# Idle products, load order, first-state banks and the order of three phases in a chunked attention + GELU-MLP kernel

## The chip, the cores and the metric

The kernel runs on one core of a Trainium2 chip. The metric is the device time of one launch in microseconds (us), from the run's start to its end on that core. The median of three runs of the kernel before is 209.88 us (209.52 to 210.0). Times inside a run are counted in us from the start of the profiled span.

## The reference

Linear attention with a per-head decay `lam`, followed by a two-layer MLP with an exact GELU. The attention output, laid out as 3072 tokens by 512 features, is the MLP's input.

```python
# q, k, v: (4 batches, 8 heads, 768, 64);  block = 64
for b in range(nb):
    intra = einsum('bhic,bhjc->bhij', qb, kb) * Dmask        # lam**(i-j) for i >= j
    intra = einsum('bhij,bhjd->bhid', intra, vb)
    inter = einsum('bhid,bhde->bhie', qb * lam_pow, kv_state)
    out[:, :, sl] = intra + inter
    kv_state = lam_block * kv_state + einsum('bhsd,bhse->bhde', kb * rev_pow, vb)
x = out.transpose(0, 2, 1, 3).reshape(3072, 512)
return gelu_exact(x @ w_in) @ w_out                          # 512 -> 2048 -> 512
```

## The kernel before

**Tiling.** The kernel works on chunks of 128 positions, six groups g = 0 to 5, each with all 4 batches (512 tokens). For each group it computes scores, masked scores, attention outputs and the state for the next group, then the first MLP product with GELU (`mm1`, 16 feature tiles of 128) and the second one (`mm2`). Groups overlap: while the MLP of group g runs, the attention of group g+1 is made. From group 2 on, the MLP products are Strassen-like: seven products in place of eight, from sums of blocks of `x`, `w_in`, `gelu` and `w_out` that VectorE makes.

**What sets the order.** Nothing is reordered by a scheduler. The kernel is recorded in the order in which its Python runs, and each engine executes its own instructions in that order, with semaphores between the engines. The order comes from strings of letters that `script` (L676) walks, one action for each word:

- `LOADS1` (L673) is the order of the DMA loads of the opening, all issued by the POOL engine. Capital V, K, Q with 0 or 1 are the halves ("pairs" of batches) of group 0; small letters those of group 1; `i0` to `i7` are eight slices of `w_in` (256 features each, `load_w_in` L109), `w0` to `w7` eight slices of `w_out` (`load_w_out` L112). `s0` and `s1` are multiplications on POOL that scale the values of pair 0 and 1 (`scale_v` L194). The halves K0 and Q0 are loaded ahead of all (L119, L120). Each pair load is two DMAs.
- `HEAD` (L674) is the work of the opening: `.` is one idle product (`keep_warm` L687: a 128x128 by 256 matmul on zeros, whose result nobody reads); `K`, `Q` transpose a pair's keys or queries on TensorE into PSUM and copy them out (`p_transposes` L308); `S` makes half of a pair's scores and masks them on VectorE (`p_scores` L326, masks L353); `O` makes a pair's outputs and scales them into `x` (`p_outputs` L356, `p_x` L371 with the VectorE product L374); `m` and `n` are the mm1 blocks of pair 0 and of pair 1 (`mm1_part` L692: eight matmuls, then GELU on ACT), in the order of slices 0, 4, 1, 5, 2, 6, 3, 7; `z` makes the first state (`p_state_products` L379, matmuls L389, VectorE L396); `g` makes ACT load the GELU table.
- `PHASE1` (L758): sixteen mm2 blocks of group 0 (`p`, `mm2_plain` L497, four rounds over four PSUM banks), sums of `w_in` and `w_out` on VectorE (`i`, `w`, `t`), and the attention of group 1 (`k`, `q`, `s`, `o`; `h` scales values on ACT).
- `PHASE2` (L777): mm1 of group 1 (`m`, `n`), attention of group 2, the states (`z`, `Z`, decay `y`, `Y` on ACT), loads of group 3 (`K`, `V`, `Q`), and the sums of `x` (`x`).
- `L2S` (L776) has sixteen digits: how many mm1 blocks later each of the sixteen VectorE sums of GELU blocks in phase 2 is recorded (`later` L63, `tick` L67).

**PSUM.** The eight banks are named by tags: uY, uV, uZ (mm1 blocks in turn), mY, mR, a0, a1, a2. A bank is free again when its reader on VectorE or ACT is done; the next writer on TensorE waits for that. The state products `z` take two banks given by their tags.

Of the kernel before, what the change touches and what calls it, by code (L numbers as in the profile page):

```python
# [14 lines left out]
def kernel(  # L15
# [11 lines left out]
    B, H, S, D = q.shape  # L27
# [20 lines left out]
    V, A, P, G, SY = nc.vector, nc.scalar, nc.tensor, nc.gpsimd, nc.sync  # L48

    def bank(tag, shape, dtype=F32, name=None):  # L50
        return ps.tile(shape, dtype, tag=tag, name=name or "p_" + tag, bufs=1)
# [4 lines left out]
    def need(*keys):  # L56
        for key in keys:
            assert key in done, key
# [28 lines left out]
    def load(g, pair, name):  # L87
        if pair == 0:
            raw[g, name] = raw_pool.tile([128, B, H, D], BF16, tag="r" + name, name="raw_" + name, bufs=1 if name == "q" else 2)
        t = raw[g, name].rearrange("p (n a) h d -> p n (a h d)", n=2)[:, pair].rearrange("p (h t d) -> p h t d", h=H, t=2)  # L90
        for b in range(2):
            G.dma_start(t[b * 64:(b + 1) * 64].rearrange("p h t d -> p h (t d)"),
                        dram[name][2 * pair + b, :, g * C:(g + 1) * C, :].rearrange("h (p t) d -> p h (t d)", t=2))
        raw[g, pair, name] = t
# [57 lines left out]
    for hi in range(2):  # L152
        p = slice(hi * D, (hi + 1) * D)
# [32 lines left out]
    def new_x(g):  # L186
        xs[g] = x_pool.tile([128, HP, B, C], BF16, tag="x", name="x_t")
# [191 lines left out]
    def p_state_products(g, tags):  # L379
        if g > 0:  # L380
            need(*[("vs", g, h) for h in range(H)])
        done.add(("sp", g))
        kv = [bank(t, [128, 2, HP, D]) for t in tags]
        for pair in range(2):
            for hp in range(HP):
                for t in range(2):
                    for b, hi in ((0, 0), (1, 1), (1, 0), (0, 1)):
                            r = slice(b * 64, (b + 1) * 64)
                            P.matmul(kv[b][hi * D:(hi + 1) * D, pair, hp, :], raw[g, pair, "k"][r, 2 * hp + hi, t, :],  # L389
                                     vs[g, pair][r, 2 * hp + hi, t, :], start=(pair == 0 and hp == 0 and t == 0),  # L390
                                     stop=True, skip_group_check=True)
        states[g + 1] = work.tile([128, B, HP, D], BF16, tag="state", name="state")
        if g == 0:
            lam_c_b = lam_c[:, None, :, None].to_broadcast((128, 2, HP, D))
            for b in range(2):
                V.tensor_mul(states[1][:, b::2], kv[b], lam_c_b)  # L396
            done.add(("st", 1))
        else:
            raw["tmp", g] = work.tile([128, B, HP, D], F32, tag="tmp", name="tmp", bufs=1)
            for b in range(2):  # L400
                V.tensor_add(raw["tmp", g][:, b::2], kv[b], states[g][:, b::2])
# [5 lines left out]
    def new_g(g):  # L407
        gts[g] = g_pool.tile([128, NK2, T], BF16, tag="g", name="g_t")
# [261 lines left out]
        return slots  # L670


    LOADS1 = "V0 K1 i0 Q1 i4 i5 i1 i2 V1 s0 i6 i3 w4 q0 i7 s1 w2 w0 k0 w1 k1 v0 w5 q1 w7 w6 v1 w3"  # L673
    HEAD = "b . . . . . . . . . . . . . . . . . . . . . . . Q K . . S S g . . . . . . O Q K m S m S m m m O z n n m m n n n n n m n"  # L674

    def script(text, actions):  # L676
        for word in text.split():
            fn = actions[word]
            (fn.pop(0) if isinstance(fn, list) else fn)()
# [12 lines left out]
    def mm1_part(g, i, pair, lag=None):  # L692

        need(*[("x", g, 2 * pair + b) for b in range(2)])
        h = bank(tags[part_no[0] % 3], [128, 2, 256])
        part_no[0] += 1
        x = xs[g].rearrange("p k s c -> p k (s c)")
        w = slice(256 * pair, 256 * pair + 256)
        for j in range(2):
            kf = 2 * i + j  # L700
            for ki in range(NK1):
                P.matmul(h[:, j, :], w_in_t[:, ki, kf * 128:(kf + 1) * 128], x[:, ki, w],  # L702
                         start=(ki == 0 and j == 0), stop=True, skip_group_check=True)
        A.activation(gts[g][:, 2 * i:2 * i + 2, w], h, ACT.Gelu)
        done.add(("gp", g, i, pair))
        u = i % 4
        if lag and all(("gp", g, x, y) in done for x in (u, u + 4) for y in range(2)):
            done.update(("g", g, u, n) for n in "XYZW")
            for n, j in enumerate((1, 2, 4, 3)):
                later(int(lag[4 * u + n]), lambda j=j: sums_g(g, u, j))  # L710
        tick()

    new_x(0)
    new_g(0)
    for item in LOADS1.split():
        i = int(item[1:])
# [6 lines left out]
        else:  # L723
            load(int(item[0].islower()), i, item[0].lower())
    script(HEAD, {
        ".": keep_warm,
# [6 lines left out]
              lambda: (p_outputs(0, 1, 0, ("a2", "a0")), p_outputs(0, 1, 1, None), p_x(0, 1, 0), p_x(0, 1, 1))],  # L733
        "m": [lambda i=i: mm1_part(0, i, 0) for i in (0, 4, 1, 5, 2, 6, 3, 7)],
        "n": [lambda i=i: mm1_part(0, i, 1) for i in (0, 4, 1, 5, 2, 6, 3, 7)],
        "z": lambda: p_state_products(0, ("a1", "a2")),
    })


# [15 lines left out]
        "z": lambda: p_state_products(1, ("a0", "a1")),  # L755
        "y": lambda: decay(2, raw["tmp", 1]),
    }
    PHASE1 = "i i p w i k q p p p w i p s q k w t p p s p t p w s o p p p h h p s p p o p"  # L758
    script(PHASE1, attn_1)


# [11 lines left out]
    new_g(1)  # L773
    new_gs(1)
    new_x(2)
    L2S = "2242369401781123"  # L776
    PHASE2 = "q z m k y n s q m n k K s h n m s V o m Q n n s t t M h c m n o c c x c x m x x m Z n m n Y"  # L777

    def digits(text, i, n):
        return [int(c) for c in text[i * n:(i + 1) * n]]  # L780

    script(PHASE2, {
        "m": [lambda i=i: mm1_part(1, i, 0, L2S) for i in (0, 4, 1, 5, 2, 6, 3, 7)],
        "n": [lambda i=i: mm1_part(1, i, 1, L2S) for i in (0, 4, 1, 5, 2, 6, 3, 7)],
        "w": attn_1["w"],
# [27 lines left out]
    for g in range(2, NG):  # L813
# [17 lines left out]
        for c in seqs:  # L831
# [6 lines left out]
            elif c == "v":  # L838
                i = visits.pop(0)
# [5 lines left out]
            elif c == "c":  # L845
                x = cross.pop(0)
                if g + 2 < NG:
                    crossbar(g + 2, *x)
            elif c == "h":
                h = heads.pop(0)  # L850
                if att:
                    scale_v_group(g + 1, h)
            elif c == "x":
                i = sums.pop(0)
# [38 lines left out]
```

## Time and profile before

| | |
|---|---|
| median of 3 runs | 209.88 us (209.52 to 210.0) |
| the profiled execution's own time | 210.69 us |
| its span, first to last instruction | 208.9 us |
| mean granted TensorE clock | 0.975 |
| TensorE (PE) busy | 196.9 us, 94% |
| VectorE (DVE) busy | 143.2 us, 69% |
| ScalarE (ACT) busy | 120.4 us, 58% |
| GpSimd (POOL) busy | 57.9 us, 28% |

How to read it: PE is the matmul stream, PEld the weight loads that overlap with it, POOL also issues the loads, SP the stores. The page's second part cuts the span into 40 slices of 5.2 us and gives the busy share of each engine in tenths; PEclk is the clock that TensorE was granted, in tenths of full speed. The views by windows give busy us and instruction counts (x) for chosen stretches. The timeline gives start and duration of merged groups of instructions, with the idle time before them and what ended it in brackets. The chain of waits follows the work that ended last back to its start.

### The profile page before, as it was taken

The numbers are of one execution on the slowest core, as the hardware profiler recorded it, in microseconds if no ns is written. First come the engines' busy times: TensorE is split into PE (matmuls) and PEld (weight loads), VectorE is DVE, ScalarE is ACT, GpSimd is POOL, SyncE is SP. The second block draws the span as 40 slices with busy tenths as digits, with TensorE's granted clock in tenths as the row PEclk, the third lists the DMA queues.
The fourth block names the chain that finished last, engine by engine and source line by source line (L and its number), as shares of the span: only waits on it lengthen the run. The fifth ranks groups of instructions, "written<-read, shape, count | busy, mean of one in ns | idle before, by whom it ended". The sixth has DMA issues, their size and how long they took to land.

```text
span 208.9 us, 6157 instructions
## 1 busy us (share of the span) xinstructions
PE 196.9 (94%) x2639; PEld 158.8 (76%) x2639; DVE 143.2 (69%) x290; ACT 120.4 (58%) x245; POOL 57.9 (28%) x70
## 2 busy tenths in 40 slices
PE   7459899999999998999999999999999999999992
PEld 5337688554678887888888888888888888888881
DVE  1872495688567996798988498796699654665140
ACT  5524446355479858872589663788455556665201
POOL 7978886775071302700035000000000000000000
PEclk9785999999999999999999999999999999999999
DMA  5999999999789945999929996330002030022123
GB/s 56 139 177 191 195 195 190 192 179 164 151 143 155 136 82 99 99 157 120 211 77 149 155 132 126 103 100 3 0 27 80 2 100 3 0 72 81 51 83 117
DMA packets 81274, 23.46 MB, mean 112 GB/s; under 512 B 69472, under 2 KB 80736, under 8 KB 81248
## 3 DMA queue, kind: packets, MB, share of 16 engines
q0 software_dynamic: 62416, 13.64, 74.3%
q1 hardware_dynamic: 18832, 9.44, 20.6%
q8 instruction: 20, 0.33, 0.7%
q14 instruction: 6, 0.05, 0.1%
HBM read 27.27 MB, written 6.29 MB: 161 GB/s over the span
## 4 chain that ended last, share of the span: by engine, by line
PE 89%; ACT 3%; DVE 2%; DMA 2%; issue 1%; POOL 1%; DVEq 0%; ACTq 0%; POOLq 0%
PE p_mY L665 15%; PE p_uY L521 14%; PE p_mR L665 13%; PE p_uV L521 7%; PE p_uV L702 5%; PE p_uY L702 5%; PE p_uZ L702 4%; PE t_ps L314 4%; PE p_uZ L521 3%; DMA raw_q<-in_q_dram 2%; PE p_a L269 2%; PE p_a L241 2%; PE p_uY L501 2%; PE p_a L347 2%; PE p_uZ L501 2%; PE p_uV L501 2%
## 5 line engine op out<-in xcount | busy, mean ns | idle before, releaser
L665 PEld LDWEIGHTS <-g_t 128*128 128x128 bf16 x320 | 31.1, 98 | 4.2 <-issue 0.4
L521 PEld LDWEIGHTS <-s_in 128*128 128x128 bf16 x256 | 24.5, 97 | 5.5 <-issue 2.2
L702 PEld LDWEIGHTS <-w_in_t 128*128 128x128 bf16 x256 | 24.8, 101 | 4.3 <-issue 0.3
L665 PEld LDWEIGHTS <-gs 128*128 128x128 bf16 x240 | 23.3, 98 | 2.9
L665 PE MATMUL p_mY<-w_out_t,g_t 128*128 128x256 bf16 x160 | 20.8, 273 | 0.2 <-ACT o_q L648 0.2
L521 PEld LDWEIGHTS <-w_in_t 128*128 128x128 bf16 x192 | 18.5, 98 | 2.8
L521 PE MATMUL p_uY<-tx,s_in 128*128 128x256 bf16 x128 | 19.2, 272 | 1.0 <-ACT p_uV L543 1.0
L533 ACT ACTIVATE g_t<-p_uV 128x512 bf16<-128x512 f32 x16 | 9.5, 594 | 17.6 <-PE p_uV L521 17.4
L571 DVE TENSOR_TENSOR p_uZ<-p_uY,Vs 128x512 f32<-128x512 f32 x16 | 11.2, 699 | 10.6 <-PE p_uY L521 10.4
L353 DVE TENSOR_TENSOR sc_m<-p_a,m_p 128x512 bf16<-128x512 f32 x20 | 12.9, 686 | 6.3 <-PE p_a L347 6.2
L259 DVE TENSOR_TENSOR sc_m<-p_a,m_p 128x512 bf16<-128x512 f32 x24 | 15.6, 683 | 1.1 <-PE p_a L244 1.1
L533 ACT ACTIVATE g_t<-Vs 128x512 bf16<-128x512 f32 x16 | 10.0, 628 | 10.1 <-DVE Vs L580 10.1
L580 DVE TENSOR_TENSOR Vs<-p_uY,Vs 128x512 f32<-128x512 f32 x16 | 11.0, 691 | 6.9 <-PE p_uY L521 6.7
L98 POOL DMA_DIRECT2D raw_q<-in_q_dram x3 | 5.1, 1704 | 32.5 <-DMA qT<-raw_q 32.5
L471 DVE TENSOR_TENSOR gs<-g_t 128x512 bf16<-128x512 bf16 x20 | 8.4, 420 | 8.0 <-ACT g_t L533 7.9
L702 PE MATMUL p_uY<-x_t,w_in_t 128*128 128x256 bf16 x88 | 12.3, 286 | 0.0
L702 PE MATMUL p_uV<-x_t,w_in_t 128*128 128x256 bf16 x88 | 12.2, 285 | 0.0
L665 PE MATMUL p_mR<-t_out,gs 128*128 128x256 bf16 x80 | 11.4, 273 | 0.0
L665 PE MATMUL p_mR<-w_out_t,g_t 128*128 128x256 bf16 x80 | 11.2, 273 | 0.0
L543 ACT COPY p_uV<-p_uY 128x512 f32<-128x512 f32 x16 | 9.2, 572 | 3.3 <-PE p_uY L521 3.2
L665 PE MATMUL p_mR<-w_out_t,gs 128*128 128x256 bf16 x80 | 11.0, 273 | 0.0
L551 ACT COPY Vs<-p_uV 128x512 f32<-128x512 f32 x16 | 9.4, 588 | 2.5 <-PE p_uV L521 2.5
(125 smaller groups left out, 434.9 us busy)
## 6 DMA issues: line engine op xcount, KB each, us to landing
w_in_t<-in_moe_w_in_dram POOLq DMA_DIRECT2D x8, 256.0 KB, 7.6
w_out_t<-in_moe_w_out_dram POOLq DMA_DIRECT2D x8, 256.0 KB, 6.9
raw_k<-in_k_dram POOLq DMA_DIRECT2D x12, 128.0 KB, 6.2
raw_q<-in_q_dram POOLq DMA_DIRECT2D x12, 128.0 KB, 5.7
raw_v<-in_v_dram POOLq DMA_DIRECT2D x12, 128.0 KB, 6.3
raw_k<-in_k_dram POOLq DMA_DIRECT2D x3, 512.0 KB, 10.6
raw_v<-in_v_dram POOLq DMA_DIRECT2D x3, 512.0 KB, 12.0
raw_q<-in_q_dram POOLq DMA_DIRECT2D x3, 512.0 KB, 9.5
```

What stands on the lines that cost most here:

```text
L259: V.tensor_mul(sc_m[g, s_sc][:, :, r, :], sc[r], m_nh[:, r])
L353: V.tensor_mul(sc_m[g, pair][half][:, :, hi], sc[hi], m_ph[:, hi, 2 * half:2 * half + 2])
L471: eng.tensor_add(s1, gLH, gHH)
L501: P.matmul(mo[io], gts[g][:, kf, io * C:(io + 1) * C], w_out_t[:, kf, :], start=(part == 0 and j == 0), stop=(part == 3 and j == 3))
L521: P.matmul(dst[:, b, :], w(ko, f0 + b * 128), x_of(ko), start=(start and b == 0 and ko == 0), stop=True, skip_group_check=True)
L533: A.activation(dst, src, ACT.Gelu)
L543: A.copy(st["V"], st["Y"])
L551: A.copy(st["Vs"], st["V"])
L571: V.tensor_add(st["Z"], st["Y"], st["Vs"])
L580: V.tensor_add(st["Vs"], st["Y"], st["Vs"])
L665: P.matmul(st[dst][:, io, :], a(kf, io), b(kf), start=(new and u == 0 and io == 0 and kf == 0), stop=True, skip_group_check=True)
L702: P.matmul(h[:, j, :], w_in_t[:, ki, kf * 128:(kf + 1) * 128], x[:, ki, w], start=(ki == 0 and j == 0), stop=True, skip_group_check=True)
```

## The change

Five edits in the opening and the two phases behind it; no computed value changes.

```diff
-    LOADS1 = "V0 K1 i0 Q1 i4 i5 i1 i2 V1 s0 i6 i3 w4 q0 i7 s1 w2 w0 k0 w1 k1 v0 w5 q1 w7 w6 v1 w3"
-    HEAD = "b . . . . . . . . . . . . . . . . . . . . . . . Q K . . S S g . . . . . . O Q K m S m S m m m O z n n m m n n n n n m n"
+    LOADS1 = "i0 V0 K1 Q1 i4 i1 i5 V1 i2 s0 i6 w4 i3 k0 s1 w0 w2 w1 i7 q0 k1 w5 v0 q1 v1 w6 w7 w3"
+    HEAD = "b . . . . . . . . . . . . . . . . . . . . . . . . K . . . . . . . . . . . . . . . Q . . . . . S . . S . g . . . . . . . . . . . O . . . . . . . . . . . . . Q K m S . S . . m m m m O z n n m n m n n n n n m n"
...
-        "z": lambda: p_state_products(0, ("a1", "a2")),
+        "z": lambda: p_state_products(0, ("mY", "mR")),
...
-    PHASE1 = "i i p w i k q p p p w i p s q k w t p p s p t p w s o p p p h h p s p p o p"
+    PHASE1 = "i p i i p w i q k p w p s q k p w p p t s t p p w s h h o p p p p s p p o p"
...
-    L2S = "2242369401781123"
-    PHASE2 = "q z m k y n s q m n k K s h n m s V o m Q n n s t t M h c m n o c c x c x m x x m Z n m n Y"
+    L2S = "1492337613340007"
+    PHASE2 = "q z m k y n s q m n s h k n K m s V o n m n t s Q t h m n c c o x c c x x Z M m m x m n n Y"
```

The idle products go from 31 to 74. Before, 23 stand ahead of the first transposes, 2 between them and the scores, and 6 ahead of the first outputs. After, 24 stand ahead of the keys of pair 0, 15 between these and the queries of pair 0, 5 ahead of the scores, 2 between the two halves of the scores, 1 + 11 ahead of the outputs of pair 0, 13 between these and the transposes of pair 1, and 1 + 2 around the second half of the scores of pair 1.

In the opening, pair 1's blocks `m` 4, 1, 5 and 2 of mm1 stand in one run ahead of `O` (three of them there before, the fourth between the two halves of the scores). In the load order `i0` moves to the front, the slices of `w_in` follow the order of their use, `V1` moves ahead of `i2`, and `i7` moves behind `k0`, `w0`, `w2` and `w1`. The number of instructions on every engine except TensorE stays as it was.

More of the change, by code (lines that the diff above doesn't have):

```diff
@@ L670, in mm2_slots @@
         return slots
-    LOADS1 = "V0 K1 i0 Q1 i4 i5 i1 i2 V1 s0 i6 i3 w4 q0 i7 s1 w2 w0 k0 w1 k1 v0 w5 q1 w7 w6 v1 w3"
-    HEAD = "b . . . . . . . . . . . . . . . . . . . . . . . Q K . . S S g . . . . . . O Q K m S m S m m m O z n n m m n n n n n m n"
+    LOADS1 = "i0 V0 K1 Q1 i4 i1 i5 V1 i2 s0 i6 w4 i3 k0 s1 w0 w2 w1 i7 q0 k1 w5 v0 q1 v1 w6 w7 w3"
+    HEAD = "b . . . . . . . . . . . . . . . . . . . . . . . . K . . . . . . . . . . . . . . . Q . . . . . S . . S . g . . . . . . . . . . . O . . . . . . . . . . . . . Q K m S . S . . m m m m O z n n m n m n n n n m n"
     def script(text, actions):
```

## The prediction

> **What bounds the kernel now.** I read the page first, for the engine that fills the span and for the clock it was granted.
>
> ```profile
> span 208.9 us, 6157 instructions
> ...
> PE   7459899999999998999999999999999999999992
> ...
> PEclk9785999999999999999999999999999999999999
> ```
>
> PE is the bound. The only slices that are not full, and the only ones below full clock, are the first five (to 26 us) and the last. So the change can win only in the opening, and lose anywhere. Then the windows, cut where the clock changes (the columns are start:end, length, busy us and instruction counts of PE, PEld, DVE, ACT and POOL, granted clock, DMA, GB/s):
>
> ```profile
> 1.05:4.46 3.41, 3.40 (x17) 2.40 (x18) 0.00 (x0) 2.09 (x3) 3.15 (x6) 1.00 0.63 60
> 4.46:7.87 3.41, 0.93 (x8) 0.59 (x6) 3.15 (x14) 2.31 (x9) 3.41 (x6) 1.00 1.41 135
> 7.87:11.29 3.42, 3.23 (x66) 2.63 (x66) 2.49 (x6) 1.98 (x5) 3.42 (x6) 0.50 1.42 141
> 11.29:14.70 3.41, 2.18 (x50) 1.25 (x42) 2.80 (x5) 0.42 (x2) 2.37 (x4) 1.00 1.56 183
> 14.70:18.11 3.41, 2.35 (x35) 2.08 (x36) 1.31 (x3) 1.07 (x2) 3.39 (x4) 0.50 1.43 191
> 18.11:21.53 3.42, 3.42 (x31) 2.10 (x29) 1.32 (x3) 1.18 (x2) 2.72 (x5) 0.50 1.61 189
> 21.53:24.94 3.41, 3.41 (x54) 2.68 (x56) 1.29 (x2) 1.84 (x4) 2.86 (x4) 1.00 1.41 196
> 24.94:28.36 3.42, 2.60 (x110) 2.28 (x103) 2.62 (x5) 0.93 (x2) 3.42 (x6) 1.00 1.52 194
> ```
>
> The clock changes in steps of 3.41 us, and each step answers to the one before it. Steps that are 27%, 64% and 69% busy (0.93, 2.18, 2.35 of 3.41) are followed by half clock; steps that are 94% or 100% busy, and the one of 76%, by full clock. DMA moves 183 to 196 GB/s from 11 us on: the loads are a queue without slack. Last, the chain of waits (start, length, what), and single rows of the timeline, for what PE waits for.
>
> ```profile
> 8.06 1.92 PE t_ps L314 x32
> ...
> 19.50 0.57 PE p_a L347 x13
> ...
> 23.98 0.87 PE p_uV L702 x8
> 24.85 0.60 PE p_a L367 x32
> ...
> 26.26 0.70 PE p_a L389 x63
> 26.96 0.98 PE p_uZ L702 x8
> ...
> 36.67 0.86 PE p_mY L501 x4
> 37.53 1.01 PE t_ps L314 x32
> 38.55 0.97 PE p_uY L501 x4
> ...
> 42.11 0.35 PE p_a L347 x16
> ```
>
> ```profile
> 6.57 2.50 DVE L167 TENSOR_TENSOR m_p<-cmask_p,lam_mp 128x512 f32<-128x512 f32 x4
> 11.18 1.29 DVE L353 TENSOR_TENSOR sc_m<-p_a,m_p 128x512 bf16<-128x512 f32 x2 [0.41 <-PE p_a L347]
> 14.90 0.72 DVE L374 TENSOR_TENSOR x_t<-p_mR,lam_q 128x512 bf16<-128x512 f32 x1
> 15.77 1.06 PE L314 MATMUL t_ps<-ident,raw_q 128*64 128x128 bf16 x16 [1.63 <-DVE x_t L374]
> 81.53 0.60 PE L521 MATMUL p_uY<-tx,s_in 128*128 128x256 bf16 x4 [0.72 <-ACT p_uV L543]
> ```
>
> From 15.77 on PE is nearly without gaps. O of pair 1 starts at 24.85, the block behind z at 26.96, phase 1 at 36.67. Those three marks carry the sum.
>
> **The change, part by part.** *Loads.* Landing is issue plus "DMA to landing". Below: the sizes, and then three pair loads, each with its row of times to landing (smallest, median, largest): K0, V1, and the second queries of group 1 (q1).
>
> ```profile
> w_in_t<-in_moe_w_in_dram POOLq DMA_DIRECT2D x8, 256.0 KB, 7.6
> w_out_t<-in_moe_w_out_dram POOLq DMA_DIRECT2D x8, 256.0 KB, 6.9
> raw_k<-in_k_dram POOLq DMA_DIRECT2D x12, 128.0 KB, 6.2
> ```
>
> ```profile
> L92 POOL DMA_DIRECT2D raw_k<-in_k_dram x2: 709/762/814, 1.3 to 2.1; - x2
> DMA to landing us min/median/max: 3.4/3.8/4.2
> L92 POOL DMA_DIRECT2D raw_v<-in_v_dram x2: 683/692/702, 12.6 to 14.1; - x2
> DMA to landing us min/median/max: 8.2/8.5/8.9
> L92 POOL DMA_DIRECT2D raw_q<-in_q_dram x2: 692/700/707, 33.2 to 33.9; - x2
> DMA to landing us min/median/max: 6.4/6.4/6.4
> ```
>
> K0 has landed at 2.1 + 4.2 = 6.3, V1 at 14.1 + 8.2 = 22.3, q1 at 33.9 + 6.4 = 40.3. As the queue has no slack, a load lands when everything listed ahead of it is through. After the change everything up to `i2` is the same set of loads as everything up to V1 was before, so i2 lands at 22.3. The block `m` on i2 started at 23.98 before, so the loads allow it to gain 1.6 and no more. q1 has only v1, w6, w7 and w3 behind it in either order of the list (before: w7, w6, v1, w3), so it stays at 40.3. Between V1 and q1 there are 8 slices of 256 KB and 10 halves of 128 KB, 26 units in 18.0 us, 0.69 each. i7 stands 16 units behind i2: 22.3 + 11.1 = 33.4. w3, last in both, stands 8 units behind q1: 45.9.
>
> *Idle products and transposes.* An idle product takes 0.21 at half clock (16 in the 3.40 of the first window), so about 0.107 at full. The 24th ends near 5.4, before K0 lands: free. Transposes of 16 cost 0.96 at half clock (1.92 for 32 at 8.06) and 0.5 at full (1.01 at 37.53). With keys from 6.4, 15 products end near 8.5 and Q0's transposes near 9.0 (Q0, next in the queue, is there 2 units of 0.69 behind K0, 7.7). But VectorE is busy with the masks' table to 9.07 (6.57 + 2.50), and then copies keys and queries out (at most 0.6 each): scores near 10.3, where the first masking began at 11.18 before. So this part gains at most 0.5 by itself, since four maskings of 0.65 follow in turn on VectorE: x of pair 0 is done near 15.1, before at 14.90 + 0.72. The products behind O fill PE until then.
>
> *Pair 1 to O.* Its transposes wait for Q1, whose set of loads is the same too (K0, Q0, V0, K1, i0, Q1) and, by 10 units behind K0 and Q0, through near 15: before, they started at 15.77, I take 15.4. V0 is 4 units behind Q0 (i0 has passed it), 10.5, and O asks for it behind 12. At full clock follow: transposes 1.0, m 0.98, two halves of S at 0.35 with three idle products 1.0, and m 4, 1, 5 at 0.98 + 0.87 + 0.87: near 21.1 (their slices land 2 units apart behind Q1, 16.8, 18.2, 19.6, and are asked for at 18.4, 19.4, 20.3). Then PE waits for i2 to 22.37. So the opening now hangs on that load, with 1.2 us of slack for everything ahead of it; if one 3.41 us step ran at half clock, the slack hides it. m takes 0.98, and O starts at 23.35 in place of 24.85: **1.50 earlier**. V1 has landed before; s1 on POOL needs 1.9 behind V1 and is done ahead of z.
>
> *The banks of z.* z no longer waits for x to leave a1 and a2. I cost this at nothing: the next block needs x of pair 1, and x starts at O's end and ended as z did (24.85 + 0.60 + two of 0.72 is 26.9, the block at 26.96). Cover gone, z's 0.70 would be exposed. The block starts at 26.96 - 1.50 = 25.46, phase 1 at 36.67 - 1.50 = 35.17. The block on i7 stands tenth: 25.46 + 0.98 + 8 x 0.87 = 33.4, as i7 lands: 0, at most 0.5.
>
> *Phase 1.* The second queries' transposes come behind p, p, q, k, p, p, s: 0.86 + 0.86 + 1.01 + 0.97 + 0.86 + 0.35 = 4.91, at 40.08, and q1 can be used at 40.46: **0.38 lost**. That leaves 1.12 (from either side: the same point stood at 41.58 in the time before, less 40.46). The ninth p needs w3 in its second half: before at 47.5 (36.67 and nine p, four transposes, two s), now 46.4, w3 at 45.9: nothing, with 0.5 to spare. h moves on ACT ahead of the copies of p's results, which come four p later: nothing.
>
> *Phase 2 and L2S.* The same products in another order. The engine that could object is VectorE:
>
> ```profile
> 65.00:80.00 15.00, 15.00 (x287) 12.72 (x285) 14.36 (x31) 12.29 (x32) 1.89 (x1) 1.00 1.62 128
> ```
>
> It has 0.64 us free in 15. Twelve of its sums (0.4 each, 31 instructions in 14.36 with the longer masks among them) now stand behind the addition for the state, eight before: 1.6 more. But Z comes three blocks of 0.87 earlier, 2.6. So 0, between a loss of 1.6 and a gain of 0.7 (the wait on ACT at 81.53, which should stay: the state's decay is still behind the last GELU).
>
> *Sum.* 1.50 - 0.38 = 1.12 off a span of 208.9: 207.8. The profiled execution took 210.69, 0.81 over the median; against the median, 209.88 - 1.12 = **208.8**.
>
> **The rivals.** *The clock drops again (209.8).* PE now idles 1.2 before i2 and, behind z (23.95 + 0.7 = 24.65), 0.8 for x. If the steps fall as before, 21.53:24.94 is idle 0.84 + 0.29, 67% busy, and steps of 64% and 69% were followed by half clock. Then of 24.94:28.36 the 2.9 us behind 25.46 do half the work: 1.45 lost, gain 0.05, no loss at q1. For it: those rows. Against: the busy part is mostly full matmuls here, while the 64% step was mostly 64-wide outputs with 50 instructions in 2.18.
>
> *The idle products do not hold the clock and stand in the way (210.8).* If the clock is half from 7.87, 6 + 5 + 2 + 12 products of 0.21, Q0 0.96 and two S of 0.57 put O at 15.2, and O's 0.6 with 13 more put pair 1's transposes near 18.5. With full clock back at 18.11, O of pair 1 starts 1.0 + 0.98 + 1.0 + 3.59 later than 18.3, at 24.9 as before; with half clock to 21.53, the transposes take 1.92 and half of the first m is slow, and it starts at 26.6, 1.75 late: 209.9 to 211.6, of which I take the middle. It decides from the point where the slack of 1.2 is used up and then the gain of 1.5. For it: two half-clock steps in a row before. Against: the run of idle products at 1.06 raised the clock at once.
>
> *The new orders give the gain back (209.7).* If Z's earlier place brings nothing, VectorE's tail of 1.6, less the 0.64 that it has free, takes 0.96 of the 1.12. For: 14.36 of 15. Against: the addition for the state stands ahead of most of the sums that phase 3 asks for late.
>
> *The Trainium skill, "TensorE: Matmul & The Clock Gate".* Its section "Why this matters for your kernels" puts a drop of the clock at idle gaps above about 3 us. By that rule the first rival falls and the sum stays at 208.8; the trace disagrees, since the clock fell at 14.70 after a step whose longest idle time (of the 1.63 before 15.77) was 0.6. Its Part 4 says that transposes do not count as busy for the clock. By that the second rival gains, as 2 us of the opening's work would not count; the trace disagrees, since 7.87:11.29 was more than half transposes (1.92 of 3.23) and was followed by full clock.
>
> **How the numbers follow.** Forecast 0.5, between 208.3 and 209.2 (landings 0.4 either way). Clock drops again 0.23 (209.4 to 210.4). Idle products in the way 0.15 (209.9 to 211.6). New orders give it back 0.12 (209.2 to 210.4). The range reaches from 208.1 to 210.7, leaving out some of the gain and most of the second rival above 210.7. A measurement of this kernel can tell 0.2%, 0.42 us, from no change. Faster is the forecast, 0.05 of the first rival and 0.03 of the third: 0.58. Same: 0.13, 0.02 and 0.05 of the three: 0.20. Slower: 0.05, 0.13 and 0.04: 0.22.
>
> **What would show it.** Right: a PE wait on the `w_in` load of about 1 us near 21 to 22, PE idle again behind z on x, phase 1 near 35.2, full clock from 11 us on, a short wait at the second queries of group 1 near 40.4, and the 0.72 at 81.5 found near 80.4. Wrong: i2 landing away from 22.3, half clock behind 22, PE reaching m on i2 after it has landed, or PE waits between 55 and 80.

## The result, and the profile after

| | before | after |
|---|---|---|
| median of 20 runs each, us | 209.82 (208.88 to 210.68) | 210.8 (209.95 to 213.08) |
| the profiled execution's own time, us | 210.69 | 211.02 |
| its span, us | 208.9 | 209.1 |
| its mean granted TensorE clock | 0.975 | 1.000 |

The ratio after to before is 1.005, with a 95% interval of 1.0027 to 1.0074: the change makes the kernel slower by half a per cent, about 1 us. The page of the kernel after:

```profile
span 209.1 us, 6243 instructions
...
PE 197.9 (95%) x2682; PEld 160.2 (77%) x2682; DVE 143.0 (68%) x290; ACT 119.9 (57%) x245; POOL 57.9 (28%) x70
...
PE   7899499999979998999999999999999999999992
...
PEclk9999999999999999999999999999999999999999
...
q8 instruction: 21, 0.34, 0.7%
```

The clock is full in every slice. Its first 5 us are to be read with care: 24 idle products took 4.71 us there, 0.20 each, and the next 15, from 6.43 on, 0.12 each. PE's row has two weak places: the fifth slice (21 to 26 us), and the twelfth (57.5 to 62.7), where the page of before has a 9. The same two lines of before, for the counts:

```profile
PE 196.9 (94%) x2639; PEld 158.8 (76%) x2639; DVE 143.2 (69%) x290; ACT 120.4 (58%) x245; POOL 57.9 (28%) x70
...
q8 instruction: 20, 0.33, 0.7%
```

The 43 added idle products are 43 matmuls and 43 weight loads, 86 instructions in all, and the queue that brings instructions (q8) carried one block more. The chain of waits of after, with the marks of the prediction in it (start, length, what):

```profile
13.57 9.35 DMA w_in_t<-in_moe_w_in_dram
...
22.96 1.05 PE p_uV L702 x8
24.01 0.60 PE p_a L367 x32
...
26.04 1.05 PE p_uZ L702 x8
...
35.82 0.86 PE p_mY L501 x4
...
40.74 1.01 PE t_ps L314 x32
...
53.21 0.59 ACT o_sb L506
53.83 4.04 DMA out_dram<-o_sb
57.96 0.59 ACT o_sb L506
58.55 0.50 ACT qT L320
...
59.09 0.64 PE t_ps L314 x16
```

O of pair 1 starts at 24.01 (before 24.85), the block behind z at 26.04 (26.96), phase 1 at 35.82 (36.67): 0.85 gained. Then the chain leaves PE, which it never did between 27 and 62 us before. It goes from a copy of phase 1's results on ACT, through their store, to another such copy, to the copy of the next queries, and back to PE at 59.09. All PE waits of after between 20 and 82 us (who, for whom: us in total, times, longest):

```profile
PE p_uV L702 <- DMA w_in_t<-in_moe_w_in_dram: 1.8, 1, 1.8
PE t_ps L314 <- ACT qT L320: 1.3, 1, 1.3
PE p_uZ L702 <- DVE x_t L374: 0.9, 1, 0.9
PE p_uY L521 <- DVE g_t L480: 0.7, 1, 0.7
```

The first, third and fourth were foreseen. The second is new. The timeline of ACT shows it, first in before, then in after:

```profile
56.21 0.59 ACT L506 COPY o_sb<-p_uV 128x512 f32<-128x512 f32 x1 [1.55 <-DMA out_dram<-o_sb]
56.81 0.59 ACT L506 COPY o_sb<-p_uZ 128x512 f32<-128x512 f32 x1
57.51 0.59 ACT L320 COPY qT<-t_ps 128x512 bf16<-128x512 bf16 x1
```

```profile
55.70 0.59 ACT L506 COPY o_sb<-p_uV 128x512 f32<-128x512 f32 x1 [1.90 <-PE p_uZ L501]
57.96 0.59 ACT L506 COPY o_sb<-p_uZ 128x512 f32<-128x512 f32 x1 [1.67 <-DMA out_dram<-o_sb]
58.44 0.59 ACT L320 COPY qT<-t_ps 128x512 bf16<-128x512 bf16 x1
```

The four results of phase 1 go through two `o_sb` buffers, so the fourth copy (`p_uZ`) waits until the second store has landed. That store took 4.04 us; before, it was issued at 54.68 and landed at 56.71, 2.03. ACT executes in order, so the copy of the queries (`qT`, L320) is queued behind the late copy. The transposes of the keys need the bank that `qT` empties, and PE stands still for 1.32 us.

What that is worth follows from two marks on PE's timeline, the first state product of phase 2 (L389) and the first block of phase 3 (L521). From the second mark to the end of the span it is 130.4 us in before and after alike. Before, and then after:

```profile
56.93 0.71 PE L389 MATMUL p_a<-vs,raw_k 64*64 64x64 bf16 x64
...
78.45 0.60 PE L521 MATMUL p_uY<-x_t,w_in_t 128*128 128x256 bf16 x4
```

```profile
56.08 0.71 PE L389 MATMUL p_a<-vs,raw_k 64*64 64x64 bf16 x64
...
59.09 0.64 PE L314 MATMUL t_ps<-ident,raw_k 128*64 128x128 bf16 x16 [1.32 <-ACT qT L320]
...
78.70 0.60 PE L521 MATMUL p_uY<-x_t,w_in_t 128*128 128x256 bf16 x4
```

The stretch between them was 21.52 us before and is 22.62 after: 1.10 lost, against the 0.85 gained ahead of it. That is the profiled span's +0.25. It leaves two questions. Why is the store late? And why is the median 1 us worse, when the profiled executions are only 0.33 apart?

A first answer to the second question lies in the executions of the kernel before that have a recorded clock, 104 of them in the experiments below. In 11 the mean clock was 0.974 to 0.976, as in the profiled one, and their median is 210.69; the other 93 are near 209.7. The profile on which the prediction was built shows a rare execution, one in ten, about 1 us slower than the others and at half clock for longer in the opening.

### The profile page after: what moved, and what is told of

Same layout as the page of the kernel before. It is cut to its first block, busy times and chain, and to the rows that moved or that the text cites. A ratio compares the mean times of both kernels' runs of the same rounds, so it can differ in the third digit from the quotient of the medians.

```text
span 209.1 us, 6243 instructions
## 1 busy us (share of the span) xinstructions
PE 197.9 (95%) x2682; PEld 160.2 (77%) x2682; DVE 143.0 (68%) x290; ACT 119.9 (57%) x245; POOL 57.9 (28%) x70
## 4 chain that ended last, share of the span: by engine, by line
PE 78%; DMA 9%; DVE 5%; POOL 3%; ACT 2%; issue 1%; POOLq 0%; ACTq 0%; DVEq 0%
PE p_mY L665 15%; PE p_uY L521 14%; PE p_mR L665 13%; DMA w_in_t<-in_moe_w_in_dram 7%; PE p_uV L521 7%; PE p_uZ L702 4%; PE p_uZ L521 3%; PE p_uV L702 3%; PE p_uY L702 3%; PE p_a L269 2%; DMA out_dram<-o_sb 2%; PE p_a L241 2%; PE t_ps L314 2%; PE p_uY L501 2%; PE p_mY L501 2%; PE p_a L244 2%
## 5 line engine op out<-in xcount | busy, mean ns | idle before, releaser
L702 PEld LDWEIGHTS <-w_in_t 128*128 128x128 bf16 x256 | 24.2, 98 | 6.4 <-DMA w_in_t<-in_moe_w_in_dram 2.1
L521 PEld LDWEIGHTS <-s_in 128*128 128x128 bf16 x256 | 24.5, 97 | 5.5 <-issue 2.2
L521 PEld LDWEIGHTS <-w_in_t 128*128 128x128 bf16 x192 | 18.5, 98 | 2.8
L521 PE MATMUL p_uY<-tx,s_in 128*128 128x256 bf16 x128 | 19.2, 272 | 1.0 <-DVE g_t L480 0.7
L571 DVE TENSOR_TENSOR p_uZ<-p_uY,Vs 128x512 f32<-128x512 f32 x16 | 11.2, 699 | 10.3 <-PE p_uY L521 10.2
L702 PE MATMUL p_uV<-x_t,w_in_t 128*128 128x256 bf16 x88 | 11.4, 273 | 1.8 <-DMA w_in_t<-in_moe_w_in_dram 1.8
L688 PE MATMUL idle_ps<-idle 128*128 128x256 bf16 x74 | 11.4, 309 | 1.1 <-DVE idle L126 1.1
L702 PE MATMUL p_uY<-x_t,w_in_t 128*128 128x256 bf16 x88 | 11.4, 273 | 0.0
L702 PE MATMUL p_uZ<-x_t,w_in_t 128*128 128x256 bf16 x80 | 10.4, 273 | 0.9 <-DVE x_t L374 0.9
```

The lines of the kernel that those rows point to most:

```text
L521: P.matmul(dst[:, b, :], w(ko, f0 + b * 128), x_of(ko), start=(start and b == 0 and ko == 0), stop=True, skip_group_check=True)
L571: V.tensor_add(st["Z"], st["Y"], st["Vs"])
L688: P.matmul(idle_ps[0][:, 0:256], idle[:, :128], idle, start=True, stop=True)
```

## The experiments

Each ratio is the time over that of the kernel before, run beside it on the same chip, with its 95% interval. It is not the quotient of the two medians and can differ from it by up to 0.2%.

**The kernel before, once more.** No edit.

> The kernel before, unchanged, to see how far its profiled execution (210.69 us, span 208.9, clock 0.975 with 10.2 us at half clock in the opening) stands for its other runs. Theory 'unlucky trace': where the 3.41 us steps of the clock fall changes from run to run; most runs spend less of the opening at half clock, the median run has a span near 208.0 and a mean clock above 0.98, and the change had about 0.9 us less to win than the trace showed. Rival: clock and span as in the first trace, 208.9 and 0.975, within 0.2; then the 0.9 us has to come from the changed kernel alone. Ratio 1.000 either way.

209.47 us in 12 runs against 210.05 in 35: 0.9968 (0.9944 to 0.9992). An identical program came out 0.3% apart, so single differences of that size say nothing here; those that follow are read together, and with their profiles. In its profile, half clock lasts 6.8 us in place of 10.2, and on PE's timeline O of pair 1 starts at 22.60 and phase 2's first state product at 55.30, both earlier than after's 24.01 (in the chain) and 56.08.

**After, with four result buffers.** The third and fourth result go through tiles that are free at that time.

```diff
-            o_sb = out_pool.tile([128, d_model], F32, tag="o", name="o_sb")
+            if io < 2:
+                o_sb = out_pool.tile([128, d_model], F32, tag="o", name="o_sb")
+            else:
+                o_sb = work.tile([128, 2, 256], F32, tag=("m_P1s", "m_Zs")[io - 2], name="o_sb", bufs=1).rearrange("p a b -> p (a b)")
```

> The changed kernel, with a buffer of its own for each of the four results that phase 1 stores (two before), so that the fourth copy on ACT waits for no store. Theory 'store': the late landing of the second store (4.04 us) holds that copy, behind it the copy of the queries, and PE for 1.32 us at 59; without it the run is 1.0 to 1.4 us faster than the changed kernel, 209.4 to 209.8, ratio to the kernel before 0.998 to 1.000, and no PE wait near 59. Rival 'orders': phases 1 and 2 would lose it anyway at the next wait; 210.5 to 210.9, ratio 1.004.

209.36 us, 0.9969 (0.9944 to 0.9995). The loss is gone: it is as fast as the kernel before once more, 209.47 beside it on the same chip. In its ACT timeline the fourth copy waits for PE's product, not for a store:

```profile
56.60 0.59 ACT L509 COPY o_sb<-p_uZ 128x512 f32<-128x512 f32 x1 [0.95 <-PE p_uZ L501]
```

The second store is late here too, 3.61 us from issue to landing, but nobody waits for it.

**Before, with four result buffers.** The same edit on the kernel before.

> The kernel before with the same four buffers. Theory 'store': in the kernel before PE does not wait for a store, so nothing changes: 209.6 to 210.0, ratio 0.999 to 1.001. Rival: the kernel before waits for stores in some of its runs as well; then it gains 0.3 or more.

209.94 us, 0.9991 (0.9964 to 1.0018). Without the change the edit is worth nothing: the copy's wait of 1.55 in the timeline above ends early enough.

**Before, with the idle products of after alone.** The loads, the banks and the phases are those of before; the 74 idle products stand as in after, keys first.

```diff
-    HEAD = "b . . . . . . . . . . . . . . . . . . . . . . . Q K . . S S g . . . . . . O Q K m S m S m m m O z n n m m n n n n n m n"
+    HEAD = "b . . . . . . . . . . . . . . . . . . . . . . . . K . . . . . . . . . . . . . . . Q . . . . . S . . S . g . . . . . . . . . . . O . . . . . . . . . . . . . Q K m S . m S . . m m m O z n n m m n n n n n m n"
```

> The kernel before with the 74 idle products in the places of the change and the keys of pair 0 first; loads, blocks, banks and the later phases stay. Theory: the clock holds from 8 us on, nothing waits for w_in (its slices land ahead of V1 here), O of pair 1 starts near 22.4 as V1 lands, 1.5 us ahead of the changed kernel; 74 products also move the instruction loads, so the second store may land late as in the changed kernel, which would give 1 us back: 208.2 to 209.4, ratio 0.992 to 0.998. Rival 'idle products in the way': 210.0 or more.

211.16 us, 1.0044 (1.002 to 1.0069): nearly the whole loss, from the idle products alone. The chain of waits of this run has the same detour as after:

```profile
52.80 0.59 ACT o_sb L506
53.42 4.33 DMA out_dram<-o_sb
...
57.85 0.58 ACT o_sb L506
58.43 0.50 ACT qT L320
...
58.97 0.64 PE t_ps L314 x16
```

The first store is late in this run too: issued at 51.66, it took 4.42 us. So the third copy also waits, to 56.48, and PE stands still twice, 0.7 us for the bank that this copy empties and 0.8 for the one that `qT` empties.

So the late store is no matter of the new loads or of the new phases. What can 86 instructions in the first 20 us do to a store at 54? They shift the blocks of 16 KB in which TensorE's instructions are brought. The DMA view counts these blocks (q8) on the same 16 engines as the stores (q1). 5278 matmuls and weight loads with 20 blocks in before are about 264 to a block, and 86 more move the later blocks forward by a third of one: the sixth starts at 54.73 in after and at 54.42 in this run, where before has it at 57.48. The view of the DMA queues from 53.5 to 56.0 us (packets, MB, share of 16 engines; q1 carries the stores), before and then after:

```profile
q1 hardware_dynamic: 234, 0.45, 47.6%
```

```profile
q1 hardware_dynamic: 214, 0.37, 40.0%
q8 instruction: 1, 0.02, 3.9%
```

Before has no block in that stretch. After has one, of 3.9% x 16 x 2.5 = 1.6 us. Read off the DMA records of eleven profiled executions, with the block nearest behind the issue of the second store (the three runs with the new loads further below are left out, as their stores run beside many more loads):

| | second store issued | block starts after | block lasts | store takes |
|---|---|---|---|---|
| before | 54.68 | 2.80 | 1.27 | 2.03 |
| before, once more | 53.05 | 2.85 | 1.49 | 2.52 |
| before, four buffers | 54.32 | 2.66 | 1.16 | 2.03 |
| before, new phases alone | 53.90 | 2.78 | 0.95 | 2.12 |
| before, wide idle products | 53.88 | 2.88 | 1.58 | 2.40 |
| after, wide idle products | 53.03 | 3.35 | 1.05 | 2.16 |
| after, 31 idle products | 53.45 | 2.76 | 1.69 | 2.01 |
| **after** | 53.83 | **0.90** | 1.57 | **4.04** |
| **after, four buffers** | 54.80 | **0.90** | 1.36 | **3.61** |
| **before, idle products alone** | 53.42 | **0.99** | 1.87 | **4.33** |
| **after, four buffers, reordered** | 54.19 | **1.31** | 0.96 | **3.74** |

The four runs with 74 narrow idle products have the block 0.9 to 1.3 us behind the issue, in the middle of the store, and their stores take 3.6 to 4.3; the seven others have it past the landing, and 2.0 to 2.5. Loads do not sort them: the store of before once more had 116 packets of loads (q0) beside it and took 2.52, that of after had 25 and took 4.04. The packets of after show the hold itself. No DMA packet at all starts between 55.60 and 56.25; then, as the block ends (54.73 + 1.57 = 56.30), six packets of q1 follow one another until 57.14, with a block of another instruction queue (q14, 8 KB, 0.51 us) beside the first of them. That second block is not needed: with four buffers none fell into the store, and it took 3.61. The reading is that the block holds up the packets of the store that stand behind it on one DMA engine, and that the store has landed only when its last packet has. On which engine a packet ran is in no view, so that part is argued.

**After, with 37 idle products of 512 columns.** About the same idle work with half the instructions.

```diff
-    idle = consts.tile([128, 256], BF16)
+    idle = consts.tile([128, 512], BF16)
...
-        P.matmul(idle_ps[0][:, 0:256], idle[:, :128], idle, start=True, stop=True)
+        P.matmul(idle_ps[0], idle[:, :128], idle, start=True, stop=True)
...
+    HEAD = "b . . . . . . . . . . . . K . . . . . . . Q . . . S . S g . . . . . . O . . . . . . . Q K m S S . m m m m O z n n m n m n n n n m n"
```

> The changed kernel with 37 idle products of 512 columns in place of 74 of 256: the same work on PE in the same places, with 74 instructions fewer. Theory 'instruction load': TensorE's instructions are loaded in blocks of 16 KB through the same DMA engines that carry the stores, and the 86 added instructions move one such load from 57.5 to 54.7, into the second store of phase 1. With the products halved it goes back to 56 to 57.5, the second store lands near 56, PE does not wait near 59, and the run is as fast as the one with four buffers: ratio to the kernel before 0.996 to 1.000. Rival 'order': the store is late for the shorter phase 1 and its neighbours, whatever the instructions: the wait of 1.3 us stays, ratio 1.004.

209.57 us, 0.9996 (0.9966 to 1.0026): the loss is gone with two buffers as well. The clock is held (mean 1.000 in the profile), and ACT's fourth copy and the copy of the queries follow with no wait for a store:

```profile
55.44 0.59 ACT L506 COPY o_sb<-p_uZ 128x512 f32<-128x512 f32 x1
55.92 0.60 ACT L320 COPY qT<-t_ps 128x512 bf16<-128x512 bf16 x1
```

But it is no gain either. All the rest of the change, with the clock held, is worth nothing that can be measured.

**After, with the 31 idle products of before in their old places.**

```diff
+    HEAD = "b . . . . . . . . . . . . . . . . . . . . . . . K Q . . S S g . . . . . . O Q K m S S m m m m O z n n m n m n n n n m n"
```

> The changed kernel with 31 idle products in the old places (23, 2 and 6; keys and queries of pair 0 next to each other). Theory: the clock falls to half for 7 to 10 us of the opening, as in the kernel before, but most of that is hidden, since PE waits for the load i2 at 23 anyway: outputs of pair 1 start at 24 to 25, at most 1 us later than in the changed kernel; the instruction load goes back and the wait at 59 is gone: ratio 0.998 to 1.003, below the changed kernel's 1.005. Rival 'the clock is what counts': outputs of pair 1 2 us later, ratio above 1.008.

209.99 us, 1.0006 (0.9978 to 1.0033), with mean clocks of 0.967 to 0.992. Without the added products the loss is gone too, and the lower clock costs the median nothing to speak of; only the three runs at 0.967 took 210.5 to 210.8.

**Before, with the new phases alone.**

```diff
-    PHASE1 = "i i p w i k q p p p w i p s q k w t p p s p t p w s o p p p h h p s p p o p"
+    PHASE1 = "i p i i p w i q k p w p s q k p w p p t s t p p w s h h o p p p p s p p o p"
-    L2S = "2242369401781123"
-    PHASE2 = "q z m k y n s q m n k K s h n m s V o m Q n n s t t M h c m n o c c x c x m x x m Z n m n Y"
+    L2S = "1492337613340007"
+    PHASE2 = "q z m k y n s q m n s h k n K m s V o n m n t s Q t h m n c c o x c c x x Z M m m x m n n Y"
```

> The kernel before with the orders of phases 1 and 2 and the digits of L2S from the change, and nothing else. Theory: they move nothing, PE stays without waits between 55 and 80, ratio 0.998 to 1.002. Rival 'orders cost': VectorE's or ACT's tail delays PE behind 55, ratio 1.004 or more.

210.19 us, 1.001 (0.9982 to 1.0039). Between phase 2's first state product and phase 3 PE needs 78.01 - 56.15 = 21.86 us, close to the 21.52 of before. The new orders cost nothing that can be told. What they do show is the wait for the second queries of group 1 that the prediction had in its sum: PE waits 0.98 us for that load here, up to 40.74.

**Before, with 37 wide idle products and keys first.** The lines of the wide product as above, and:

```diff
+    HEAD = "b . . . . . . . . . . . . K . . . . . . . Q . . . S . S g . . . . . . O . . . . . . . Q K m S . m S m m m O z n n m m n n n n n m n"
```

> The kernel before with its clock held: 37 idle products of 512 columns spread over the opening as in the change, keys of pair 0 first, everything else as before. It has 12 instructions more on TensorE, not 86, so the instruction load stays clear of the second store. It prices the clock by itself. Theory 'loads': half clock in the opening is hidden, since O of pair 1 waits for V1 and phase 1 for the loads of w_out and of the second queries; only runs with about 10 us at half clock (mean clock under 0.978, 11 of 82) lose 1 us. So ratio 0.996 to 1.001. Rival 'clock': each step at half clock costs; the kernel before has two in most runs, so 1.2 us or more are won, ratio 0.990 to 0.994.

209.37 us, 0.9988 (0.9964 to 1.0011); mean clocks of 0.996 and more. Holding the clock through the opening, with no late store, brings at most about 0.8 us by that interval, and 0.25 by its middle. Three of its PE waits from 20 to 82 us show where the early start goes:

```profile
PE p_a L367 <- DMA raw_v<-in_v_dram: 0.3, 1, 0.3
PE t_ps L314 <- DMA raw_q<-in_q_dram: 0.3, 1, 0.3
PE p_mY L501 <- DMA w_out_t<-in_moe_w_out_dram: 0.3, 1, 0.3
```

V1 (at 22.55), a load of `w_out` (at 35.18) and the second queries of group 1 (at 41.00) are each waited for in turn. Whoever comes early waits for loads.

**After, four buffers, with O of pair 1 ahead of the block on i2, and loads in the order of their use.**

```diff
-    LOADS1 = "i0 V0 K1 Q1 i4 i1 i5 V1 i2 s0 i6 w4 i3 k0 s1 w0 w2 w1 i7 q0 k1 w5 v0 q1 v1 w6 w7 w3"
+    LOADS1 = "i0 V0 K1 Q1 i4 i1 i5 V1 i2 s0 i6 i3 i7 s1 k0 w4 w0 w2 w1 q0 k1 q1 w5 v0 v1 w6 w7 w3"
...
+    HEAD = "b . . . . . . . . . . . . . . . . . . . . . . . . K . . . . . . . . . . . . . . . Q . . . . . S . . S . g . . . . . . . . . . . O . . . . . . . . . . . . . Q K m S . S . . m m m O m z n n m n m n n n n m n"
```

> The changed kernel with four result buffers, with O of pair 1 ahead of the block on i2, and with loads moved to their use: i3, i7 and s1 ahead of k0, q1 ahead of w5. Theory 'O waits for the wrong load': in the changed kernel O of pair 1 stands behind a block that needs i2, the last load of the set; placed ahead of it O starts as V1 lands, near 21.2 in place of 24, and the block behind z at 24.6 in place of 26.0; i7 and q1 are then in time, and the gain of 1.2 to 1.5 stays to the end: ratio to the kernel before 0.989 to 0.994, the fastest so far. Rival: the next load or buffer takes it back, ratio 0.996 as with four buffers alone.

210.34 us, 1.0029 (1.0 to 1.0058): a miss. O of pair 1 does start at 21.10. But w3, still last in the list, becomes the wait, in the chain of this run:

```profile
39.15 7.65 DMA w_out_t<-in_moe_w_out_dram
...
46.84 0.38 PE p_mY L501
```

PE has waited 1.23 us there, and phase 2's first state product stands at 56.44, within the 55.30 to 56.93 of the two executions of before.

**Before, with q1 and w3 loaded earlier and w4, w6 and w7 used later.** Loads and phase 1 change, nothing else.

```diff
-    LOADS1 = "V0 K1 i0 Q1 i4 i5 i1 i2 V1 s0 i6 i3 w4 q0 i7 s1 w2 w0 k0 w1 k1 v0 w5 q1 w7 w6 v1 w3"
+    LOADS1 = "V0 K1 i0 Q1 i4 i5 i1 i2 V1 s0 i6 i3 i7 s1 k0 w0 w1 q0 k1 q1 w4 w5 w2 w3 v0 v1 w6 w7"
...
-    PHASE1 = "i i p w i k q p p p w i p s q k w t p p s p t p w s o p p p h h p s p p o p"
+    PHASE1 = "i p i i p i q k p p s q k p w p p w t s t p p s h h o p p p p w s p p w o p"
```

> The kernel before with the loads behind V1 in the order of their need (q1 ahead of w4, w5, w2, w3, these ahead of v0, v1) and the sums of w_out later in phase 1, so that neither PE nor VectorE waits for a load between 34 and 50; opening, idle products and banks as before. Theory 'loads': what phase 1 waits for in the faster half of the runs goes away, 0.5 to 1.2 us: ratio 0.994 to 0.998. Rival: the loads are no bound, ratio 1.000.

212.23 us in 6 runs, 1.0131 (1.0097 to 1.0165): another miss, and the late store in a larger form. Phase 2's first state product comes early, at 54.75, but the stores now run beside loads; the source line of the stores (time to landing, smallest, median, largest) and the third copy on ACT:

```profile
DMA to landing us min/median/max: 4.5/5.4/6.0
```

```profile
57.01 0.59 ACT L506 COPY o_sb<-p_uV 128x512 f32<-128x512 f32 x1 [4.53 <-DMA out_dram<-o_sb]
```

PE waits 2.18 us for the bank that this copy empties (`p_uV`), and its clock falls after that (below). The stretch to phase 3 takes 25.23 us.

**After, four buffers, O ahead of i2, and these loads and this phase 1.** The `HEAD` and the four buffers of the reordered run, and the new `LOADS1` with i0 first:

```diff
+    LOADS1 = "i0 V0 K1 Q1 i4 i1 i5 V1 i2 s0 i6 i3 i7 s1 k0 w0 w1 q0 k1 q1 w4 w5 w2 w3 v0 v1 w6 w7"
+    PHASE1 = "i p i i p i q k p p s q k p w p p w t s t p p s h h o p p p p w s p p w o p"
```

> The changed kernel with four result buffers, O of pair 1 ahead of the block on i2, and the loads behind V1 and the sums of w_out in phase 1 in the order of their need. Theory 'loads': phase 1 starts near 34.3 as in the run before with O moved, and now keeps it: w3 lands near 40 in place of 46.8, no wait above 0.3 between 34 and 56, phase 2 near 54.4: ratio 0.990 to 0.994. Rival: another wait takes it, ratio 0.997 or more.

208.54 us (208.13 to 210.77) in 12 runs, 0.9964 (0.9929 to 0.9998): the fastest kernel here, though by less than expected. Six of its 12 runs lie below the lowest of the 22 runs of before beside it (208.69). As an identical kernel came out 0.3% apart, the size of its gain is open. Its source line of the stores, and the fourth copy on its ACT timeline:

```profile
DMA to landing us min/median/max: 4.5/5.3/5.6
```

```profile
54.58 0.59 ACT L509 COPY o_sb<-p_uZ 128x512 f32<-128x512 f32 x1 [0.95 <-PE p_uZ L501]
```

The stores are as slow as in the run above; the copy waits for PE's product and not for a store.

**The same orders with two buffers and wide idle products.**

> The same with the two result buffers of the change and 37 wide idle products in place of 74. Theory 'instruction load' and 'loads' together: as fast as the one with four buffers, ratio 0.990 to 0.995. Rival: a shorter phase 1 brings the stores under the last loads again, a wait of 1 us or more near 58, ratio 0.996 to 1.000.

212.71 us in 6 runs, 1.0153 (1.0121 to 1.0185). ACT's copy waits 4.13 us for a store, PE 1.77 for ACT. The wide products alone cost nothing (0.9996, 0.9988), so this wait comes with the missing buffers. It is less than half of the loss of 4 us against the run above: PE also halts for 0.76 us inside a block of mm1 (up to 68.33) and for 1.24 inside the state products (up to 75.35), waiting for nothing that the profile shows ("issue"). Where these two halts come from stays open.

## Why the prediction was wrong

All profiled executions, by the two marks on PE, say where time was won and lost:

| | phase 2's first state product, us | from there to phase 3, us |
|---|---|---|
| before | 56.93 | 21.52 |
| before, once more | 55.30 | 21.56 |
| before, four buffers | 56.57 | 21.52 |
| before, new phases alone | 56.15 | 21.86 |
| before, wide idle products | 56.13 | 21.52 |
| **after** | 56.08 | **22.62** |
| **before, idle products alone** | 55.67 | **23.20** |
| after, four buffers | 57.06 | 21.23 |
| after, wide idle products | 55.28 | 21.72 |
| after, 31 idle products | 55.70 | 21.75 |
| after, four buffers, reordered | 56.44 | 21.24 |
| after, four buffers, new loads | 55.04 | 21.59 |
| before, new loads, two buffers | 54.75 | 25.23 |
| after, new loads, two buffers, wide idle products | 54.99 | 25.58 |

The first column varies by about 1.8 us from one execution to the next among kernels that cannot be told apart, and not by the clock alone: the latest, 57.06, is at full clock. The second is 21.2 to 21.9 wherever no copy is kept by a store long enough to stop PE, and 22.6 to 25.6 where one is.

**What held.** The argument on the loads (the same set ahead of i2 as was ahead of V1) put PE's wait ahead of the block on i2, and that wait came: 1.8 us, the block at 22.96 against 22.37 predicted. O of pair 1 followed at 24.01 (predicted 23.35), the block behind z at 26.04 (25.46), phase 1 at 35.82 (35.17), all late by the same 0.6. That much is within what this load varies: at the same place in the list, PE had it at 22.96 here, at 23.14 with four buffers and at 21.62 with wide idle products, where the prediction allowed 0.4 either way. The second queries' transposes came at 40.74 (40.46), with no wait: coming 0.6 later, PE no longer met the load, and the 0.38 of the sum fell away. The banks of z are worth nothing, as costed: from O to the block behind z it takes 2.1 us before and after (24.85 to 26.96, 24.01 to 26.04). Keys first and the new places of the idle products are hidden in the slack ahead of i2, which was 1.8 where 1.2 was predicted. The new phases and digits are worth nothing that can be told (1.001). At phase 2 the prediction put PE 1.12 ahead of the profiled execution of before, at 55.81; it was there at 56.08, 0.85 ahead.

**First failed step: "against the median, 209.88 - 1.12 = 208.8".** The gain was worked out against an execution that took 0.81 over the median, and then taken off the median. But that 0.81 lies in the same place as the gain. The executions of before at mean clocks of 0.974 to 0.976 are the ones at 210.69, and the profiled one had 10.2 us of half clock between 7.87 and 21.53. Those at 0.979 to 0.992 (83 of 104) stand near 209.65, and the ten at 0.999 or 1.000 at 209.93, no better. So up to about 7 us of half clock is hidden behind the loads, the 1 us goes with a third step of 3.41 us, and the usual execution had little or nothing to win: in the other profile of before O of pair 1 stands at 22.60, ahead of where after puts it. That the 1 us goes with the half clock is read from which executions are slow. The wide idle products test it from the other side: with the clock held, the ratio is 0.9988. Taken off the profiled execution's own time, the prediction's sum would have been 210.69 - 1.12 = 209.6, no change.

**Second failed step: the idle products costed as "free".** They were looked at where they are executed, and the sum had no term for the stores of phase 1. Their cost lies 35 us later: 86 instructions more put a block of instructions into the second store, and the store gates ACT's fourth copy, the queries' copy behind it, and PE. The size is 22.62 - 21.52 = 1.10 us. The prediction's own sign of error, "PE waits between 55 and 80", is what appeared. The "nothing" for the new order of phase 1 stands: alone it costs nothing that can be told. Four arms carry the cause: the idle products alone bring the loss (1.0044), fewer instructions for about the same idle work take it away (0.9996), so does the old number (1.0006), and so do two more buffers with every product in place (0.9969). That it is the block's place, and not something else about the 86 instructions, rests on the table of eleven executions and on the packets of after; a kernel with as many instructions and the block moved was not run.

With both steps mended the sum is 210.69 - 1.12 + 1.10 = 210.7, where the median is 210.8. For the profiled execution of after, 210.69 - 0.85 + 1.10 = 210.94 against 211.02 is no second proof, since both terms were read from that trace.

**The rivals.** Neither drop of the clock happened in the profiled execution, and in 17 of the 20 runs of after the mean clock was 0.996 or more; the three others, at 0.988 to 0.992, took 212.5 to 213.1, and where their clock fell is in no profile. The rival in which the idle products stand in the way named the right part and the right time (210.8), but by a mechanism that did not occur: PE reached the block on i2 early, not late. That the time agrees is luck. The loss by VectorE's tail, the third, isn't seen: the wait at the start of phase 3 stayed at 0.7, though it now ends on VectorE (0.73, up to 81.77) where it ended on ACT before (0.72, up to 81.53).

## What to carry to other kernels

Before taking a gain off the median, ask whether the profiled execution's excess over the median lies in the very stretch that the change mends; if so, take it off the profiled time. An instruction that does nothing useful still has to be brought to its engine, and what it shifts can show far from where it is executed: prefer few large dummy operations to many small ones. Where a store's landing frees a buffer for the next copy, look at what is queued behind that copy on its engine, and give it buffers until a store of twice the usual length harms nobody.

## What the runs showed of the hardware

**A block of instructions in the middle of a store can nearly double it.** The second 256 KB store took 2.0 to 2.5 us with no block in its way and 3.6 to 4.3 with one of 1.0 to 1.9 us that started 0.9 to 1.3 behind its issue. A block is not the only thing that slows a store: the first store, which runs beside more loads, took 2.8 to 3.7 with none in its way, and in the three runs with the new loads the stores took 3.8 to 6.0.

**The share of busy time alone does not foretell the clock.** Windows of after, of the run with new loads and two buffers, and of before once more (start:end, length, busy us and counts of PE, PEld, DVE, ACT and POOL, granted clock, DMA, GB/s):

```profile
21.19:24.60 3.41, 1.64 (x65) 1.36 (x69) 0.00 (x0) 1.15 (x2) 3.41 (x4) 1.00 1.38 197
24.60:28.01 3.41, 2.50 (x81) 2.19 (x67) 3.34 (x7) 0.66 (x3) 3.25 (x5) 1.00 1.50 195
```

```profile
54.59:58.00 3.41, 1.23 (x78) 1.08 (x73) 1.84 (x4) 0.59 (x2) 2.21 (x2) 1.00 1.12 189
58.00:61.41 3.41, 3.41 (x30) 2.26 (x28) 0.42 (x1) 2.32 (x5) 1.17 (x1) 0.50 1.35 147
```

```profile
14.01:17.42 3.41, 1.68 (x50) 1.39 (x49) 1.53 (x4) 0.54 (x2) 3.40 (x4) 1.00 1.46 197
17.42:20.84 3.42, 3.42 (x57) 2.59 (x56) 2.47 (x5) 2.12 (x5) 2.73 (x5) 1.00 1.60 189
```

In after PE was 48% busy in one such stretch, and wherever one lays steps of 3.41 us over 8 to 36 us, one of them is under 64% busy; the clock stayed full, where before it fell behind steps of 64% and 69%. In the second run it fell behind a step of 36% with a wait of 2.18 us. In the third it stayed full behind a step of 49%, in the same kernel whose clock fell behind 64% and 69%. So the prediction's reading, that each step answers to how busy the one before it was, does not hold, and the one step of transposes that it names cannot tell whether transposes count. What decides stays open. The Trainium skill, "TensorE: Matmul & The Clock Gate", section "Why this matters for your kernels", puts the drop at idle gaps above about 3 us: the waits of 1.77 and 0.91 in after agree with that, the drop behind 2.18 does not.

**Identical kernels vary early, not late.** From the first block of phase 3 to the end it took 130.4 to 130.5 us in all fourteen profiled executions; up to phase 2 the two executions of the kernel before differ by 1.6 us (56.93 and 55.30).
